# Seven-segment second products for every pair of units, with g's sums made by accumulating DMAs

## The chip, the cores and the metric

The kernel runs on one core of one Trainium2 chip. The metric is the device time of one execution in microseconds (us); the median of several runs counts. A core has a matrix engine (PE, with its weight loads shown as PEld), a vector engine (DVE), an activation engine (ACT), GpSimd (POOL), a queue engine that issues DMAs (SP), and 16 DMA engines that all queues share.

## The reference

Two blocks follow one another. The first is a chunked state-space scan over x (4 batches, 8 heads, 768 steps, 32 channels) with decay `a` and projections B and C (16 states). The second takes the scan's result as 3072 tokens of 256 values through two matrix products with a SiLU between them:

```python
x = attn_out.transpose(0, 2, 1, 3).reshape(B * S, H * D)   # 3072 x 256
h = x @ w_in                                               # 256 x 2048
g = h * (1.0 / (1.0 + np.exp(-h)))
out = g @ w_out                                            # 2048 x 256
```

All is float32.

## The kernel before

**Units and pairs.** The 3072 tokens are cut into 12 units of 256 tokens. For each unit the scan produces XM (the unit's 256 inputs, transposed), the first product gives g in a tile GTS[u] ("gT" in the profile, 128 partitions x 16 blocks of 256), and the second product reads it. Two units form a pair P. Four buffers hold g tiles.

**Seven products in place of eight.** A pair's second product can be seen as a 2 x 2 block product, with blocks of w_out and four blocks of g: b11 and b21 from the pair's first unit, b12 and b22 from its second, where the first index is the half of the 2048 (block number even or odd). Done directly it takes eight block products; with sums of blocks formed beforehand seven are enough. The kernel does the pairs 1 to 5 that way: `s2_pair` (L559) yields after each of 7 segments x 8 matmuls of 128 x 256. The sums of w_out blocks (SO, `f_SO`, L512) are made once on DVE. The sums of g blocks are TN and three in-place ones, made by `f_TS` (L534), each as eight subtractions of 128 x 256, on POOL (the last pair's late ones on DVE). Pair 0, that is units 0 and 1, does its second product directly in `s2_list` (L490): 2 units x 2 halves x 16 matmuls. The first product of units 4 to 11 also has seven segments (`f_x1`, L647), with sums SW of w_in blocks (`f_SW`, L623, POOL) and XT of inputs (`f_XT`, L634, POOL); units 0 to 3 use the direct `f_s1` (L475).

**Order.** Every engine's order is written out by hand. First comes a start-up part in which PE also runs matmuls without use (`busy`, L218), so that it isn't idle. Then w_in and w_out are brought into a reduced form piece by piece (`w_size` on ACT, `w_bits` on DVE and POOL), beside the scans and first products of units 0 to 2. Two loops of eight steps follow, one for unit 2's first product (L838, called loop 1 below) and one for unit 3's (L853, loop 2). Each step takes four PE matmuls of `f_s1` and four of the second product by `f_s2(4)`, and the scan pieces of units 3 (loop 1) and 4, 5 (loop 2): "T" transposes, "E" the decay scans, "B"/"D"/"C" products on POOL, "G" the score matmuls with the state updates `f_S` and the mask products `f_M` on DVE, "Y" the scan's output matmuls and XM. Last come stages G = 2 to 5 (L868), one for each pair's first product: a step j of `f_x1` interleaves its seven matmuls with seven of the previous pair's second product (the "s" in `ORDER`). A final loop (L894) does the last pair alone.

**Queues and buffers that matter.** The scan's scores and output share one PSUM tile "gy" with a single buffer: `f_M` reads the scores there, and `f_Y` (L444) then writes the same place:

```python
nc.vector.tensor_tensor(out=m[:, k], in0=DP[u][:, :, 128 * k:128 * k + 128], in1=m[:, k], op=ALU.mult)
y = ps_s.tile([128, 4, 512], FP32, name="gy")
```

The second product's PSUM tile "o_ps" has one buffer; it is emptied by ACT copies to "ps" tiles (five buffers), which POOL adds (`p_add`, L544) into outputs that DVE transposes and SP stores (`f_out`, L547). SP also issues all loads of a unit (`load_unit`, L124).

Of the kernel before, what the change touches and what calls it, by code (L numbers as in the profile page):

```python
# [21 lines left out]
def kernel(  # L22
# [22 lines left out]
    nc = tc.nc  # L45
# [196 lines left out]
    busy(4, 14)  # L242
# [230 lines left out]


    def f_s1(g, j):  # L475
        if j == 0:
            GTS[g] = gpool.tile([128, NF, UT], FP32, name="gT")
        xm = XM[g].rearrange("p (w c) t -> p w (c t)", w=2)
        hp = ps_h.tile([128, 2, UT], FP32, name="hp")
        for i in range(2):  # L480
            f = 2 * j + i
            for kc in range(KC):
                nc.tensor.matmul(out=hp[:, i], lhsT=w_in_sb[:, kc, f * 128:(f + 1) * 128],  # L483
                                 rhs=xm[:, kc], start=(kc == 0), stop=(kc == KC - 1))
        nc.scalar.activation(GTS[g][:, 2 * j:2 * j + 2], hp, AF.Silu)  # L485
        if j == 7:
            XM.pop(g)


    def s2_list(units):  # L490
        for g in units:
            b, t0 = at(g)
            r = out[b * S + t0:b * S + t0 + UT].rearrange("(k c i) m -> k i c m", k=2, c=2)
            o = ps_o.tile([128, 2, d_model], FP32, name="o_ps")
            for c in range(2):
                for f in range(NF):
                    nc.tensor.matmul(out=o[:, c], lhsT=GTS[g][:, f, 128 * c:128 * c + 128], rhs=w_out_sb[:, f, :],  # L497
                                     start=(f == 0), stop=(f == NF - 1), skip_group_check=True)
                    if f == NF - 1 and c == 1:
                        for e in range(2):  # L500
                            o_sb = ppool.tile([128, UT], FP32, name="ps")
                            nc.scalar.activation(o_sb, o[:, e], AF.Copy)
                            for k in range(2):
                                nc.sync.dma_start(out=r[k][:, e], in_=o_sb[64 * k:64 * k + 64])
                    yield

# [3 lines left out]
    SO, TN, PEND = [], {}, []  # L510

    def f_SO(i):  # L512
# [4 lines left out]
        def new():  # L517
            if i == 3:
                return lo(spare(None, 128))
            return [wtp.tile([128, 2, WF], FP32, name=n).rearrange("p a (b m) -> p (a b) m", m=128)  # L520
                    for n in ("wu", "wv")]

        SO.append(new())
        b = lambda k, m: lo(wjo[:, k, m])
        a0, a1, op = ((b(0, 1), b(1, 1), ALU.add), (SO[0], b(0, 0), ALU.subtract),
                      (b(0, 0), b(0, 1), ALU.subtract), (b(1, 0), SO[min(i, 1)], ALU.subtract))[i]
# [3 lines left out]
    def gb(P, k, v):  # L530

        return GTS[2 * P + v].rearrange("p (j k) t -> p k j t", k=2)[:, k]

    def f_TS(P, i, q, engine):  # L534


        if i == 0 and q == 0:
            TN[P] = tpool.tile([128, NF // 2, UT], FP32, name="TN")
        b11, b21, b12, b22 = gb(P, 0, 0), gb(P, 1, 0), gb(P, 0, 1), gb(P, 1, 1)
        o, a0, a1 = ((TN[P], b12, b11), (b11, b22, TN[P]), (b12, b22, b12), (b21, b21, b11))[i]  # L540
        for j in (2 * q, 2 * q + 1):
            engine.tensor_tensor(out=o[:, j], in0=a0[:, j], in1=a1[:, j], op=ALU.subtract)  # L542

    def p_add(o, p, q, engine):  # L544
        engine.tensor_tensor(out=o, in0=p, in1=q, op=ALU.add)  # L545
# [13 lines left out]
    def s2_pair(P, final=False):  # L559
# [3 lines left out]
                ("5", lambda j: SO[0][j // 4][:, j % 4], lambda: TN[P]),  # L563
                ("6", lambda j: SO[1][j // 4][:, j % 4], lambda: gb(P, 0, 0)),
                ("7", lambda j: SO[2][j // 4][:, j % 4], lambda: gb(P, 0, 1)),
                ("4", lambda j: wjo[:, 1, 1, j], lambda: gb(P, 1, 0)),
                ("3", lambda j: SO[3][j // 4][:, j % 4], lambda: gb(P, 1, 1)))
        for n, (m, w, g) in enumerate(segs):
            if final and n % 2 == 0:
# [3 lines left out]
            for j in range(NF // 2):  # L573
                nc.tensor.matmul(out=o, lhsT=w(j), rhs=g()[:, j], start=(j == 0), stop=(j == NF // 2 - 1))  # L574
                if j == NF // 2 - 1:

                    p[m] = ppool.tile([128, UT], FP32, name="ps")
                    on = o.rearrange("p (c k t) -> p c k t", c=2, k=2)
                    pn = p[m].rearrange("p (k c t) -> p c k t", c=2, k=2)
                    if not (final and m == "3"):  # L580
                        nc.scalar.activation(pn, on, AF.Copy)  # L581
                    if m == "w":
                        p_add(p["w"], p["w"], p["1"], adder)
                        PEND.append(partial(f_out, P, 0, 0, p["w"]))
                    elif m == "6":
                        p_add(p["6"], p["6"], p["1"], adder)
                    elif m == "7":
                        p_add(p["7"], p["7"], p["6"], adder)
                        p_add(p["6"], p["6"], p["5"], adder)
                        p_add(p["5"], p["5"], p["7"], adder)  # L590
                        PEND.append(partial(f_out, P, 1, 1, p["5"]))
                    elif m == "4":
                        p_add(p["4"], p["4"], p["7"], adder)
                        PEND.append(partial(f_out, P, 1, 0, p["4"]))
                    elif m == "3" and final:

                        for k in range(2):
                            nc.vector.tensor_tensor(out=pn[:, :, k], in0=on[:, :, k],
                                                    in1=p["6"].rearrange("p (k c t) -> p c k t", c=2, k=2)[:, :, k],
                                                    op=ALU.add)  # L600
                            f_out(P, 0, 1, p["3"], (nc.sync, nc.scalar), (128 * k, 128 * k + 128))
                    elif m == "3":
                        p_add(p["3"], p["3"], p["6"], adder)
                        PEND.append(partial(f_out, P, 0, 1, p["3"]))
# [18 lines left out]
    def f_SW(i):  # L623
# [5 lines left out]
        nc.gpsimd.tensor_tensor(out=t, in0=a0, in1=a1, op=op)  # L629
# [17 lines left out]
    def f_x1(G, j, dve, act):  # L647
        u0, u1 = 2 * G, 2 * G + 1
        if j == 0:
            for u in (u0, u1):  # L650
                GTS[u] = gpool.tile([128, NF, UT], FP32, name="gT")
# [23 lines left out]
        for what in ORDER[j]:  # L675
# [5 lines left out]
            elif what == "1":  # L681
                mm(X, wj[:, 0, 0, j], b0[:, 0])
                p1 = copy("p1", X)
                add(g0[:, 2 * j], W, p1)
# [4 lines left out]
            elif what == "6":  # L689
                mm(X, SW[1][:, j], t[:, 1], False)  # L690
                u2 = copy("u2", X)
                silu(g0[:, 2 * j], g0[:, 2 * j])
                other(dve, first)
            elif what == "7":
                mm(X, SW[2][:, j], t[:, 2], False)
                add(g1[:, 2 * j + 1], X, p5)
                silu(g1[:, 2 * j + 1], g1[:, 2 * j + 1])
            elif what == "4":
                mm(X, wj[:, 1, 1, j], t[:, 3], False)
                silu(g0[:, 2 * j + 1], X)  # L700
                other(dve, 2)
            elif what == "3":
                mm(Y, SW[3][:, j], b1[:, 1], False)
                add(g1[:, 2 * j], Y, u2)
                silu(g1[:, 2 * j], g1[:, 2 * j])
# [66 lines left out]
    busy(0, 24)  # L772
    f_G0(0)
    busy(4, 10)
# [14 lines left out]
    busy(3, 30)  # L789
# [47 lines left out]
    S2.append(s2_list((0, 1)))  # L837
    for j in range(8):  # L838
        f_s1(2, j)
        scan_piece(3, j, ("", "", "T", "E", "BS", "G", "S", "Y"))  # L840
        f_s2(4)
        if j < len(late):
            w_steps(late[j])
        if j in (2, 5):
            load_unit(4 + j // 3)

    def sums(P, qs):

        for q in qs:
            f_TS(P, 0, q, nc.gpsimd)  # L850
            f_TS(P, 2, q, nc.gpsimd)

    for j in range(8):  # L853
        f_s1(3, j)
# [78 lines left out]
```

## Time and profile before

| | us |
|---|---|
| median of 11 runs | 357.24 |
| lowest, highest | 356.71, 359.27 |
| the profiled execution: its time | 357.97 |
| the profiled execution: its span | 356.2 |

About 1.8 us of a run lie outside the span. Some groups of the page's fifth part (line, engine, operation, tiles and shape, count, then busy us and mean ns of one, then the idle time before):

```profile
L483 PE MATMUL hp<-XM,w_in_sb 128*128 128x256 f32 x256 | 59.3, 381 | 0.7 <-ACT XM L472 0.7
L497 PE MATMUL o_ps<-w_out_sb,gT 128*128 128x256 f32 x128 | 30.9, 384 | 0.0
L545 POOL TENSOR_TENSOR ps<-ps 128x256 f32<-128x256 f32 x28 | 20.3, 728 | 25.9 <-ACT ps L581 12.7
```

A float32 matmul stands in the profile as two records, so the 128 records of L497 are 64 matmuls. Records overlap, as matmuls are pipelined: the mean ns of one record is longer than the distance between two, and busy time is counted without overlap.

### The profile page before, as it was taken

The page shows a single profiled execution, that of the slowest core. Times are in us where ns is not written, and L with a number is a line of the kernel's source. Part 1 is how long each engine was busy: PE and PEld are TensorE (multiplying, and loading weights), DVE is VectorE, ACT ScalarE, POOL GpSimd, SP SyncE. Part 2 cuts the span into 40 slices and gives each one's busy share as a digit, 9 for nine tenths or more (in the row PEclk, how much of TensorE's full clock was granted, in tenths as well). Part 3 has the DMA queues.
Part 4 walks back from the last instruction along what each step waited for, and adds up shares of the span by engine and source line. Part 5 has one row for each costly group of instructions (what it writes and reads, how often), then busy time and mean ns, then how long its engine had stood idle before and what let it go on. Part 6 is the DMA issues. An engine that isn't in the chain of part 4 may idle for free.

```text
span 356.2 us, 8462 instructions
## 1 busy us (share of the span) xinstructions
PE 346.7 (97%) x3353; PEld 292.0 (82%) x3353; DVE 183.4 (51%) x389; ACT 160.4 (45%) x390; POOL 181.7 (51%) x246
## 2 busy tenths in 40 slices
PE   8799999999999999999999999999999999999994
PEld 4478888888888888888888888888888888888883
DVE  6988999554447444543454633455632221214722
ACT  2469576223222545545544545544545454453100
POOL 4425344524059086498274398264398930596100
PEclk9999999999999999999999999999999999999998
DMA  6998967773653251252026153110101100101203
GB/s 107 217 346 136 284 211 129 126 119 72 114 124 45 67 97 17 46 99 37 15 61 106 38 97 45 18 16 2 17 2 16 17 15 0 17 0 21 41 0 45
DMA packets 110059, 26.53 MB, mean 74 GB/s; under 512 B 98884, under 2 KB 105796, under 8 KB 110020
## 3 DMA queue, kind: packets, MB, share of 16 engines
q1 hardware_dynamic: 107044, 25.67, 35.0%
q10 hardware_dynamic: 2976, 0.33, 0.6%
q8 instruction: 26, 0.43, 0.5%
q14 instruction: 13, 0.11, 0.1%
HBM read 22.83 MB, written 3.15 MB: 73 GB/s over the span
## 4 chain that ended last, share of the span: by engine, by line
PE 92%; DMA 2%; DVE 2%; issue 1%; SPq 0%; ACT 0%; ACTq 0%; DVEq 0%
PE o_ps L574 30%; PE hp L657 28%; PE hp L483 15%; PE o_ps L497 8%; PE hp L574 3%; PE gy L463 3%; PE gy L454 2%; PE gy L400 2%; DMA gT<-in_a_dram 1%; PE gy L385 1%; DVE E L411 1%; DMA tbc<-in_B_dram 1%; DVE st L426 0%; DMA out_dram<-ot 0%; DVE gT L275 0%
## 5 line engine op out<-in xcount | busy, mean ns | idle before, releaser
L660 DVE TENSOR_TENSOR gT<-hp,p 128x256 f32<-128x256 f32 x64 | 26.9, 421 | 84.6 <-ACT p L671 47.5
L483 PE MATMUL hp<-XM,w_in_sb 128*128 128x256 f32 x256 | 59.3, 381 | 0.7 <-ACT XM L472 0.7
L663 ACT ACTIVATE gT<-gT 128x256 f32<-128x256 f32 x96 | 39.7, 414 | 42.8 <-DVE gT L660 42.8
L336 POOL TENSOR_TENSOR BT<-bn,E 128x256 f32<-128x256 f32 x12 | 8.8, 736 | 95.1 <-PE hp L657 29.7
L574 PE MATMUL o_ps<-gT,w_out_sb 128*128 128x256 f32 x224 | 56.5, 379 | 0.0
L483 PEld LDWEIGHTS hp<-XM,w_in_sb 128*128 128x128 f32 x256 | 48.1, 190 | 8.1 <-issue 0.9
L657 PE MATMUL hp<-raw 128*128 128x256 f32 x192 | 52.7, 380 | 0.0
L542 POOL TENSOR_TENSOR gT<-gT 128x256 f32<-128x256 f32 x72 | 51.2, 739 | 0.0
L574 PEld LDWEIGHTS o_ps<-gT,w_out_sb 128*128 128x128 f32 x224 | 42.4, 190 | 5.9
L657 PEld LDWEIGHTS hp<-raw 128*128 128x128 f32 x192 | 36.2, 190 | 5.4 <-POOL ps L545 0.6
L671 ACT ACTIVATE p<-hp 128x256 f32<-128x256 f32 x64 | 24.6, 384 | 27.5 <-PE hp L657 25.7
L485 ACT ACTIVATE gT<-hp 128x512 f32<-128x512 f32 x32 | 19.1, 596 | 39.3 <-PE hp L483 39.2
L660 DVE TENSOR_TENSOR gT<-hp,u 128x256 f32<-128x256 f32 x32 | 13.6, 425 | 40.7 <-PE hp L657 40.7
L657 PE MATMUL hp<-XM,w_in_sb 128*128 128x256 f32 x128 | 34.1, 389 | 0.0
L545 POOL TENSOR_TENSOR ps<-ps 128x256 f32<-128x256 f32 x28 | 20.3, 728 | 25.9 <-ACT ps L581 12.7
L497 PE MATMUL o_ps<-w_out_sb,gT 128*128 128x256 f32 x128 | 30.9, 384 | 0.0
L542 POOL TENSOR_TENSOR TN<-gT 128x256 f32<-128x256 f32 x40 | 28.7, 740 | 0.0
L497 PEld LDWEIGHTS o_ps<-w_out_sb,gT 128*128 128x128 f32 x128 | 23.8, 190 | 3.8 <-issue 0.5
L657 PEld LDWEIGHTS hp<-XM,w_in_sb 128*128 128x128 f32 x128 | 23.3, 190 | 4.3 <-issue 1.0
L299 DVE TENSOR_TENSOR_SCAN E<-ab,diag 128x256 f32<-128x256 f32 (+1 forms) x32 | 24.5, 805 | 3.7 <-PE gy L463 3.3
L542 POOL TENSOR_TENSOR gT<-gT,TN 128x256 f32<-128x256 f32 x32 | 22.2, 733 | 0.0
L581 ACT ACTIVATE ps<-o_ps 128x256 f32<-128x256 f32 x31 | 11.9, 384 | 18.5 <-PE o_ps L574 18.1
(123 smaller groups left out, 548.7 us busy)
## 6 DMA issues: line engine op xcount, KB each, us to landing
ab<-in_a_dram SPq DMA_DIRECT2D x40, 128.0 KB, 3.4
raw<-in_moe_w_in_dram SPq DMA_DIRECT2D x8, 512.0 KB, 8.7
raw<-in_moe_w_out_dram SPq DMA_DIRECT2D x8, 512.0 KB, 5.7
xt<-in_x_dram SPq DMA_DIRECT2D x24, 128.0 KB, 4.2
out_dram<-ot SPq DMA_DIRECT2D x76, 32.0 KB, 1.7
bn<-in_B_dram SPq DMA_DIRECT2D x22, 64.0 KB, 5.4
tbc<-in_C_dram SPq DMA_DIRECT2D x40, 32.0 KB, 1.9
pa<-in_a_dram SPq DMA_DIRECT2D x10, 128.0 KB
```

Source lines behind the costliest of these rows:

```text
L299: nc.vector.tensor_tensor_scan(out=E[u].rearrange("p k h t -> p (k h t)")[:, Q * g0:Q * (g0 + n)], data0=t.rearrange("p g t -> p (g t)"), ...
L483: nc.tensor.matmul(out=hp[:, i], lhsT=w_in_sb[:, kc, f * 128:(f + 1) * 128], rhs=xm[:, kc], start=(kc == 0), stop=(kc == KC - 1))
L485: nc.scalar.activation(GTS[g][:, 2 * j:2 * j + 2], hp, AF.Silu)
L497: nc.tensor.matmul(out=o[:, c], lhsT=GTS[g][:, f, 128 * c:128 * c + 128], rhs=w_out_sb[:, f, :], start=(f == 0), stop=(f == NF - 1), skip_ ...
L542: engine.tensor_tensor(out=o[:, j], in0=a0[:, j], in1=a1[:, j], op=ALU.subtract)
L545: engine.tensor_tensor(out=o, in0=p, in1=q, op=ALU.add)
L574: nc.tensor.matmul(out=o, lhsT=w(j), rhs=g()[:, j], start=(j == 0), stop=(j == NF // 2 - 1))
L581: nc.scalar.activation(pn, on, AF.Copy)
L657: nc.tensor.matmul(out=o, lhsT=w, rhs=x_, start=start, stop=True, skip_group_check=True)
L660: nc.vector.tensor_tensor(out=o, in0=p, in1=q, op=ALU.add)
L663: nc.scalar.activation(o, i, AF.Silu)
L671: nc.scalar.activation(o, i, AF.Copy)
```

## The change

- Pair 0's second product is also done by `s2_pair`, with `joint=True`: its first two segments run block by block side by side in the two halves of one PSUM tile, the other five one after the other. `s2_list` is gone. Loop 1 and loop 2 take 2 or 4 matmuls of it in a step, 28 in each.
- The signs of the sums are changed so that all sums of g are additions in place: TN = b12 + b11 (`f_T1`, DVE, in four parts of 128 x 512), then b12 += b22 ("3"), b11 += b12 ("2"), b21 += b11 ("4"). The in-place ones are DMAs with `accum_op`, issued on POOL's queue, each in two halves of 512 KB; the last pair's late ones are DVE or POOL additions of 128 x 1024. The segments "6" and "7" change places.
- g's layout in its tile becomes half first, block second (`new_g`), so that four blocks of a half lie together.
- SW is made on DVE, and spread over loop 2. SO is made in loop 1 (three) and loop 2 (one). Unit 3's scan pieces move: transposes to the end of step 2, "DC" in step 4, "G" at the end of step 6, and "Y" after the first product of step 7 and ahead of the second product's matmuls. Loads are issued after a step's outputs.
- `busy` counts change: (4, 14) to (5), (0, 24) to (0, 20), (4, 10) to (4, 8), (3, 30) to (4, 17), where the first number counts matmuls of 512 columns and the second of 64.

```diff
-    busy(4, 14)
+    busy(5)
...
+    def new_g():
+        return gpool.tile([128, NF, UT], FP32, name="gT").rearrange("p (k j) t -> p k j t", k=2)
...
-        nc.scalar.activation(GTS[g][:, 2 * j:2 * j + 2], hp, AF.Silu)
+        nc.scalar.activation(GTS[g][:, :, j], hp, AF.Silu)
...
+    def f_T1(P, q, engine=nc.vector):
+        if q == 0:
+            TN[P] = tpool.tile([128, NF // 2, UT], FP32, name="TN")
+        js = slice(2 * q, 2 * q + 2)
+        engine.tensor_tensor(out=TN[P][:, js], in0=gb(P, 0, 1)[:, js], in1=gb(P, 0, 0)[:, js], op=ALU.add)
+
+    def f_TS(P, i, h, engine=None):
         b11, b21, b12, b22 = gb(P, 0, 0), gb(P, 1, 0), gb(P, 0, 1), gb(P, 1, 1)
-        o, a0, a1 = ((TN[P], b12, b11), (b11, b22, TN[P]), (b12, b22, b12), (b21, b21, b11))[i]
-        for j in (2 * q, 2 * q + 1):
-            engine.tensor_tensor(out=o[:, j], in0=a0[:, j], in1=a1[:, j], op=ALU.subtract)
+        js = slice(4 * h, 4 * h + 4)
+        o, a = {3: (b12, b22), 2: (b11, b12), 4: (b21, b11)}[i]
+        if engine is None:
+            nc.gpsimd.dma_start(out=o[:, js], in_=a[:, js], accum_op=ALU.add)
+        else:
+            engine.tensor_tensor(out=o[:, js], in0=a[:, js], in1=o[:, js], op=ALU.add)
...
+    def s2_pair(P, final=False, joint=False):
...
+            elif m == "6":
+                p_add(p["6"], p["6"], p["1"], adder)
+                p_add(p["7"], p["7"], p["6"], adder)
+                p_add(p["6"], p["5"], p["6"], adder, ALU.subtract)
+                p_add(p["5"], p["5"], p["7"], adder, ALU.subtract)
+                PEND.append(partial(f_out, P, 1, 1, p["5"]))
...
+        if joint:
+            o = ps_o.tile([128, 2, UT], FP32, name="o_ps")
+            for j in range(NF // 2):
+                for n, (m, w, g) in enumerate(segs[:2]):
+                    nc.tensor.matmul(out=o[:, n], lhsT=w(j), rhs=g()[:, j], start=(j == 0 and n == 0), stop=(j == last),
+                                     skip_group_check=True)
+                    if j == last and n == 1:
+                        end("1", o[:, 0])
+                        end("w", o[:, 1])
+                    yield
...
-        nc.gpsimd.tensor_tensor(out=t, in0=a0, in1=a1, op=op)
+        nc.vector.tensor_tensor(out=t, in0=a0, in1=a1, op=op)
...
-    busy(0, 24)
+    busy(0, 20)
     f_G0(0)
-    busy(4, 10)
+    busy(4, 8)
...
-    busy(3, 30)
+    busy(4, 17)
...
-    S2.append(s2_list((0, 1)))
+    def outputs(todo):
+        for what in todo:
+            what()
+
+    S2.append(s2_pair(0, joint=True))
     for j in range(8):
+        waiting, PEND[:] = PEND[:], []
         f_s1(2, j)
-        scan_piece(3, j, ("", "", "T", "E", "BS", "G", "S", "Y"))
-        f_s2(4)
+        if j == 7:
+            scan_piece(3, 0, "Y")
+        f_s2(2 if j < 2 else 4)
         if j < len(late):
             w_steps(late[j])
+        if j == 2:
+            scan_piece(3, 0, "T")
+            for q in range(4):
+                f_T1(0, q)
+        if j == 3:
+            f_SO(0)
+        scan_piece(3, j, ("", "", "", "E", "DC", "", "G", ""))
+        if j in (5, 6):
+            f_SO((2, 1)[j - 5])
+        outputs(waiting)
...
+        for h in range(2):
+            if j in (3, 5, 7):
+                f_TS(0, {3: 3, 5: 2, 7: 4}[j], h)
...
     for j in range(8):
         f_s1(3, j)
-        scan_piece(4, j, ("TE", "BS", "G", "Y", "", "", "", ""))
-        scan_piece(5, j, ("", "", "T", "E", "BS", "G", "Y", ""))
+        scan_piece(4, j, ("TE", "DCS", "G", "YS", "", "", "", ""))
+        scan_piece(5, j, ("", "", "T", "E", "DCS", "G", "YS", ""))
...
-        f_s2(4)
+        f_s2(2 if j in (5, 6) else 4)
+        if j == 3:
+            f_SO(3)
+        outputs(waiting)
         if j == 5:
-            sums(1, (0, 1))
+            f_T1(1, 0)
+            f_T1(1, 1)
+            f_TS(1, 3, 0)
...
+            if j < 2:
+                f_T1(G - 1, 2 + j)
+            for i, h in {1: ((2, 0), (3, 1)), 2: ((2, 1),), 3: ((4, 0), (4, 1))}.get(j, ()):
+                f_TS(G - 1, i, h)
+            if j == 5:
+                f_T1(G, 0)
+                f_T1(G, 1)
+                f_TS(G, 3, 0)
...
-    sums(P, (3,))
+    f_T1(P, 2)
+    f_T1(P, 3)
+    f_TS(P, 3, 1, nc.gpsimd)
     S2.append(s2_pair(P, True))
...
-            for q in range(4):
-                f_TS(P, 2 * n + 1, q, nc.vector)
+            for h in range(2):
+                f_TS(P, 2 * n + 2, h, nc.vector)
```

## The prediction

> **What bounds the kernel.** I read the page's busy times and its chain first, then busy time by stage (cut where the loops begin), then PE's waits, then the timelines around the places that the change moves.
>
> ```profile
> PE 346.7 (97%) x3353; PEld 292.0 (82%) x3353; DVE 183.4 (51%) x389; ACT 160.4 (45%) x390; POOL 181.7 (51%) x246
> PE 92%; DMA 2%; DVE 2%; issue 1%; SPq 0%; ACT 0%; ACTq 0%; DVEq 0%
> ```
>
> The chain that ended last is PE for 92% of the span, and the other engines are half idle. By stage (start:end, length, busy us of PE, PEld, DVE, ACT, POOL, granted clock, DMA share, GB/s):
>
> ```profile
> 0.00:27.42 27.42, 22.82 (x437) 14.76 (x438) 21.82 (x45) 12.21 (x25) 10.68 (x23) 1.00 0.87 227
> 53.10:83.52 30.42, 30.42 (x283) 26.11 (x281) 20.57 (x34) 10.91 (x21) 11.87 (x9) 1.00 0.70 118
> 83.52:116.87 33.35, 33.35 (x442) 28.08 (x441) 17.52 (x30) 9.61 (x20) 18.06 (x18) 1.00 0.47 89
> 116.87:170.72 53.85, 53.85 (x537) 45.94 (x536) 24.84 (x61) 27.41 (x74) 34.48 (x51) 1.00 0.32 60
> ```
>
> These are the start-up, loop 1, loop 2 and stage G = 2. PE is busy without a gap from 27.42 us until the last matmul (about 351); the only idle PE time is in the start-up. So a matmul taken out behind 27.42 us shortens the run by its full length, unless PE is made to wait somewhere new. Its length comes from the chain of waits: "327.16 3.45 PE hp L574 x16" is one segment, 16 records or 8 matmuls: 0.431 us each. (Check: loops 1 and 2 last 63.8 us; their 128 matmuls take 55.2, and the rest is two to three units' scan matmuls.)
>
> **Pair 0 in seven segments.** Out go L497's 64 matmuls, in come 7 x 8 = 56: 8 x 0.431 = **-3.45 us**, all on PE's path. The number of `f_s1` and scan matmuls stays.
>
> **Sums of g.** POOL loses 144 operations of L542 at 0.73 to 0.74 us, 102 us of its 182. It was no bound, so this gains nothing. DVE gets 24 `f_T1` of 128 x 512. The nearest row is L528, the same shape from SBUF to SBUF on DVE: 0.67 to 1.21 us each, so 16 to 29 us in all. In stages 2 to 5 four of them (2.7 to 4.8 us) come on top of DVE's 25 of 54 us (12 of 49 in the last). Each stands at the end of a step, and behind it waits the step's first g addition (L660), which only has to free a PSUM buffer for the step after. Cost 0; with that cover gone, one `f_T1`'s length (1.2 us) in a step.
>
> In the last loop DVE does four additions of 128 x 1024 instead of 16 of 128 x 256 (7.0 us), and POOL one (L629 has that shape: 2.35 us). Segment "7" needs the POOL result three segments (10.4 us) after the stage; two `f_T1` and that addition take under 5. Cost 0. The tail behind the last matmul is unchanged.
>
> **The accumulating DMAs** are the large unknown: 31 of 512 KB. The trace has none. Nearest row by size:
>
> ```profile
> raw<-in_moe_w_out_dram SPq DMA_DIRECT2D x8, 512.0 KB, 5.7
> ```
>
> 5.7 us to landing, up to seven in line; the DMA view over 22.7 to 24 us shows 389 GB/s, thus 1.35 us of the rings for one. An accumulation has to read two streams and write one. I take two to three times 1.35, that is 2.7 to 4 us each (estimate). Allowance: a stage issues b11 (first half) and b12 (second half) behind step 1, the other half of b11 behind step 2, both of b21 behind step 3. Steps last 54 / 8 = 6.7 us and carry seven second-product matmuls. The fourth of these DMAs is needed at matmul 40, in step 5, some 24 us behind step 1: 6 us each even if all ran one after the other. Cost 0; the loss begins at 6 us each.
>
> The Trainium skill has rules that speak against this step. "DMA: Bandwidth & Descriptors" (Rules for kernel authors) says that an accumulation's destination isn't held while it is read and written back, so that dependent ones must wait for each other's semaphores: b12, then b11, then b21, with POOL's queue standing still at each wait. "SBUF — State Buffer" (SBUF: two separate sides) says that DMAs issued from GpSimd can't write their descriptors while DVE holds the shared port. The trace agrees that DVE and POOL get in each other's way: L176's 128 x 512 pass takes 0.43 us at 25.33 and 1.39 at 29.98, beside a POOL addition. But such a hold lasts one operation, about 1 us: 6 holds a stage would use 6 of the 24 us, while without the rule they use none. Both leave the sum at 0. Behind POOL's waits stand unit products (L336), output additions and XT, all needed a step or more later.
>
> **SW and SO.** Four SW of 128 x 1024 go from POOL (2.35 us) to DVE: twice L528, 1.3 to 2.4 us each, and three SO go from loop 2 to loop 1. DVE's loop 1 by its rows: last weight piece done at about 61.5; transposes 1.2, four `f_T1` 3.3 (66), SO 1.6 (67.7), unit 3's decay scan 4.1 (71.8). PE wants TN and SO at 70.4 and the scan's result (plus 0.7 for L336) at about 75.5. Both hold by 2.5 us. In loop 2 the same count leaves DVE 1 to 2 us ahead of unit 5's "G" with the short durations and 1.5 us late with the long ones. POOL is emptier now, so I take the short ones: 0, with +1.5 as the far end.
>
> **Unit 3's Y is moved too near to its G.** In loop 1 of before:
>
> ```profile
> 72.67 0.69 PE L400 MATMUL gy<-ce,bh 32*64 32x128 f32 x32
> 73.47 0.23 DVE L424 COPY st<-gy 128x64 f32<-128x64 f32 x1 [5.93 <-PE gy L400]
> 73.73 0.91 DVE L426 SCALAR_TENSOR_TENSOR st<-st,pfx,gy 128x64 f32<-128x64 f32 x3
> 74.56 1.28 DVE L411 TENSOR_TENSOR E<-gy,E 128x512 f32<-128x512 f32 x2
> ...
> 80.39 0.58 PE L454 MATMUL gy<-cw,sm 32*64 32x64 f32 x24
> ```
>
> G's matmuls give PE free at 73.29; DVE then needs until 75.84 for states and masks, and Y may not write "gy" sooner. Before, Y came 7.1 us behind G. Now G ends step 6, and between it and Y stands only step 7's first product: 4 x 0.431 = 1.73 us. Needed: 75.84 - 73.29 = 2.55, plus 0.1 from DVE's end to PE's start (unit 1: 24.96 to 25.11). PE waits **+0.9 us**, once. Units 4 (cover 3.45) and 5 (cover 2.6, with a shorter state update that needs 2.3) don't wait.
>
> **The start-up.** One wait there has no releaser:
>
> ```profile
> PE gy L463 <- issue: 2.2, 1, 2.2
> PE o_ps L221 <- DVE gT L216: 1.3, 1, 1.3
> PE hp L483 <- ACT XM L472: 0.7, 1, 0.7
> PE gy L454 <- DVE E L411: 0.4, 2, 0.3
> ```
>
> PE stops in the middle of unit 0's Y (14.43 to 16.61 us). The DMA view over 13.9 to 15.4 us has one 16 KB packet on an instruction queue, beside rings that are busy with weights; the next is at 22.8, the next at 28.1. I read this as PE running out of code. The new `busy` counts take out 31 of 89 matmuls (62 instructions), so the code present reaches 62 instructions further: past the remaining 25 of Y's matmuls, into unit 0's first product, which can't start before its weights at 16.3 anyway. Y(0) then ends at 14.9, not 17.0. DVE begins unit 1's scan 0.3 us sooner (its weight pieces end at 16.86), PE reaches unit 1's state matmuls at 20.7 instead of 21.94, and Y(1) starts about 1.2 us sooner. But the next chunk of code, present from about 25.2 us if its packet comes when it did, is now first needed inside Y(1), at 24.8: 0.5 us are lost again. Net **-0.7 us**. From the two sides: -1.2 if the second chunk is in time; +1.3 if its fetch is asked for by position in the code and not by time, for then the whole 2.2 us hole stands in Y(1), on the path. I take the middle one because both packets are served late, in step with the rings' load.
>
> **The sum** on the profiled execution: span 356.2 - 3.45 + 0.9 - 0.7 = 352.95; with the 1.8 us outside, 354.7 against its 357.97. The median of the runs is 0.7 below that execution, so 357.24 - 3.25 = **354.0 us**.
>
> **Rivals.**
> - *No new waits (0.15).* PE hides Y(3) because step 7's silu and DVE overlap better than I count, and the second chunk is in time: 357.24 - 3.45 - 1.2 = 352.6. For it: DVE is half idle. Against it: the gy buffer's single copy.
> - *Given back (0.13).* The hole moves into Y(1) (+1.3), Y(3) waits (+0.9), and DVE, crowded by SW at its long durations, is late for unit 5 (+1.5): 357.24 + 0.25, about 357.5. For it: the DVE stretch of 17.5 us in loop 2 would grow to about 25.
> - *The accumulating DMAs decide (0.16), slower.* In stages 2 to 5 PE waits at segments "6" and "4" if one takes over 6 us. At 6.6 us the fifth comes about 3.5 us late in each of four stages: 354.0 + 14 = 368. For it: no such transfer is in the trace, and POOL stands in line for each. Against it: the rings are 67 to 93% idle there.
>
> **The numbers.** The forecast has 0.56, with its own range 353.2 to 355.2. Runs of this kernel tell about 0.3% (1.07 us) from no change. Faster: 0.56 + 0.15 + 0.04 of the third case's spread = 0.75. Same: 0.07, the middle of that case. Slower: 0.16 + 0.02 = 0.18. The 8-in-10 range goes from the second case's end, 352.4, to the third's, 357.3; what lies above is mostly the DMAs' case.
>
> **What would show it.** L497 gone and 672 records of second-product matmuls in all (112 a pair, six pairs); loops 1 and 2 together about 61.2 us, that is 63.8 - 3.45 + 0.9; a PE wait of 0.9 on DVE L411 ahead of L454 in unit 3; no "issue" wait in unit 0's Y, a short one in unit 1's; first matmul of unit 1's first product at about 26.7 instead of 27.42; stages of 53.9 us as before, with no PE wait on a DMA. Wrong would be: stages longer than 54 us with PE waiting for gT (the DMAs), or a start-up later than 27.4.

## The result and the profile after

The changed kernel takes 355.04 us (median of 13 runs, 354.53 to 356.96), the kernel before 357.46 beside it: a ratio of 0.9923, with a 95% interval of 0.9903 to 0.9944. That is faster by 2.4 us, by the medians, where I forecast 3.25; the interval of the ratio stands for 2.0 to 3.5 us, so the two can't be told apart by the times alone, and what follows compares terms in the profiles. The profiled execution took 354.87 us, its span is 353.2 (before: 356.2).

The page of the changed kernel, busy times, a DMA queue that before did not have, the chain, and one DMA issue row (KB each, median us to landing):

```profile
PE 342.3 (97%) x3306; PEld 287.1 (81%) x3306; DVE 205.9 (58%) x409; ACT 162.0 (46%) x393; POOL 112.0 (32%) x137
...
q0 software_dynamic: 4464, 16.25, 24.9%
...
PE 91%; DVE 4%; DMA 2%; issue 1%; ACT 0%; POOL 0%; SPq 0%; ACTq 0%; DVEq 0%
...
gT<-gT POOLq DMA_DIRECT2D x31, 512.0 KB, 6.1
```

PE has 47 records fewer: 16 are the 8 matmuls of pair 0, 31 are `busy` matmuls. POOL has lost 70 us and PE's share of the chain is what it was, so POOL's 70 us were not on the path as such. The new queue holds the rings for 24.9% of 353.2 us, 88 us for 31 transfers, thus 2.84 us of all rings each; from issue to landing one takes 6.1.

Busy time by stage (start:end, length, busy us of PE, PEld, DVE, ACT, POOL, granted clock, DMA share, GB/s); the rows are the start-up, loop 1, loop 2 and stage G = 2:

```profile
0.00:26.23 26.23, 21.80 (x407) 13.22 (x407) 21.64 (x45) 12.33 (x25) 11.06 (x23) 1.00 0.87 229
51.90:82.30 30.40, 29.70 (x279) 25.44 (x278) 26.41 (x44) 12.06 (x24) 13.64 (x14) 1.00 0.89 157
82.30:112.87 30.57, 30.57 (x429) 25.61 (x428) 21.99 (x33) 9.88 (x21) 15.40 (x15) 1.00 0.80 134
112.87:166.75 53.88, 53.88 (x537) 45.83 (x536) 28.00 (x66) 27.24 (x73) 15.78 (x22) 1.00 0.80 141
```

Read against the rows of before, this says where the 3.0 us of span are. Up to loop 1 it is 1.2 us earlier (53.10 to 51.90). The two loops last 60.97 us in place of 63.77: 2.80 less. From stage 2 to the last matmul it is 234.19 against 234.09, no change, although the rings in stage 2 are now busy 80% of the time where they were 32%. From the start of the last matmul to the end it is 6.09 against 5.26, 0.83 lost. 1.2 + 2.8 - 0.1 - 0.83 = 3.07.

PE's waits in the changed kernel (waited for: us in total, times, longest):

```profile
PE o_ps L221 <- DVE gT L216: 1.3, 1, 1.3
PE hp L487 <- POOL w_in_sb L182: 1.3, 2, 1.0
PE gy L454 <- ACT gT L489: 0.7, 1, 0.7
PE hp L487 <- ACT XM L472: 0.7, 1, 0.7
PE gy L400 <- ACT ce L361: 0.6, 1, 0.6
PE gy L454 <- DVE E L411: 0.5, 1, 0.5
```

The 2.2 us with no releaser are gone; a smaller hole is left in unit 1's Y (below). In their place stand waits for a weight piece (L182) and for CE (L361), both in the start-up. No row names a DMA or a sum of g. The third row is the new wait in loop 1; its surroundings in the timeline:

```profile
74.92 0.69 PE L400 MATMUL gy<-ce,bh 32*64 32x128 f32 x32
...
76.82 1.28 DVE L411 TENSOR_TENSOR E<-gy,E 128x512 f32<-128x512 f32 x2
...
78.25 0.58 PE L454 MATMUL gy<-cw,sm 32*64 32x64 f32 x24 [0.70 <-ACT gT L489]
```

This is unit 3: scores, masks, then Y. The masks on "gy" end at 78.10 and Y starts 0.15 later, the same distance as in unit 1 of before; the silu that the view names (L489, 77.58 to 78.18) ends at nearly the same time. Which of the two holds Y is tried below.

### The profile page after: what moved, and what is told of

It reads as the page before. It is cut to its first block, busy times and chain, and to the rows that moved or that the text cites. A ratio compares the mean times of both kernels' runs of the same rounds, so it can differ in the third digit from the quotient of the medians.

```text
span 353.2 us, 8347 instructions
## 1 busy us (share of the span) xinstructions
PE 342.3 (97%) x3306; PEld 287.1 (81%) x3306; DVE 205.9 (58%) x409; ACT 162.0 (46%) x393; POOL 112.0 (32%) x137
## 3 DMA queue, kind: packets, MB, share of 16 engines
q0 software_dynamic: 4464, 16.25, 24.9%
## 4 chain that ended last, share of the span: by engine, by line
PE 91%; DVE 4%; DMA 2%; issue 1%; ACT 0%; POOL 0%; SPq 0%; ACTq 0%; DVEq 0%
PE o_ps L614 35%; PE hp L669 28%; PE hp L487 15%; PE hp L614 3%; PE gy L463 3%; PE o_ps L600 2%; PE gy L454 2%; PE gy L400 2%; DVE E L299 1%; PE gy L385 1%; DVE wv L178 1%; DMA tbc<-in_C_dram 1%; DMA tbc<-in_B_dram 1%; DMA out_dram<-ot 0%; DVE gT L275 0%
## 5 line engine op out<-in xcount | busy, mean ns | idle before, releaser
L614 PE MATMUL o_ps<-gT,w_out_sb 128*128 128x256 f32 x240 | 60.4, 379 | 0.0
L540 POOL TENSOR_TENSOR ps<-ps 128x256 f32<-128x256 f32 x35 | 29.4, 839 | 73.8 <-ACT ps L571 72.5
L614 PEld LDWEIGHTS o_ps<-gT,w_out_sb 128*128 128x128 f32 x240 | 45.4, 190 | 6.3
L535 POOL DMA_DIRECT2D gT<-gT x31 | 27.2, 914 | 67.3 <-DVE TN L526 21.5
L489 ACT ACTIVATE gT<-hp 128x512 f32<-128x512 f32 x32 | 19.1, 596 | 30.1 <-PE hp L487 29.9
L299 DVE TENSOR_TENSOR_SCAN E<-ab,diag 128x256 f32<-128x256 f32 (+1 forms) x32 | 25.6, 843 | 0.4
L571 ACT ACTIVATE ps<-o_ps 128x256 f32<-128x256 f32 x38 | 14.5, 383 | 23.9 <-PE o_ps L614 21.0
L336 POOL TENSOR_TENSOR BT<-bn,E 128x256 f32<-128x256 f32 x12 | 9.5, 793 | 46.7 <-DVE E L299 41.4
L614 PE MATMUL o_ps<-gT,wu 128*128 128x256 f32 x88 | 22.2, 380 | 0.0
L614 PE MATMUL o_ps<-gT,wv 128*128 128x256 f32 x88 | 22.2, 380 | 0.0
L614 PE MATMUL o_ps<-gT,raw 128*128 128x256 f32 x80 | 20.6, 382 | 0.0
L669 PE MATMUL hp<-raw,w_in_sb 128*128 128x256 f32 x64 | 19.1, 380 | 0.0
```

The source lines that it names most:

```text
L299: nc.vector.tensor_tensor_scan(out=E[u].rearrange("p k h t -> p (k h t)")[:, Q * g0:Q * (g0 + n)], data0=t.rearrange("p g t -> p (g t)"), ...
L489: nc.scalar.activation(GTS[g][:, :, j], hp, AF.Silu)
L535: nc.gpsimd.dma_start(out=o[:, js], in_=a[:, js], accum_op=ALU.add)
L540: engine.tensor_tensor(out=o, in0=p, in1=q, op=op)
L669: nc.tensor.matmul(out=o, lhsT=w, rhs=x_, start=start, stop=True, skip_group_check=True)
```

## The experiments

Unless said otherwise each is the changed kernel with one edit; "before" is run beside each on the same chip.

### What pair 0's seven segments are worth

`pair0_direct`: pair 0's second product in 64 matmuls again, no sums for it.

```diff
-    S2.append(s2_pair(0, joint=True))
+    S2.append(s2_list((0, 1)))
...
-        f_s2(2 if j < 2 else 4)
+        f_s2(4)
```

> The changed kernel with pair 0's second product done directly, 64 matmuls instead of 56, four in each step of both loops; pair 0's sums of g are left out, everything else as changed. Theory (a matmul on PE's path costs its full 0.431 us): 3.45 us longer than the changed kernel, 358.5, all of it in the two loops. Rival (the seven segments bring waits of their own, so that part of the gain is given back in the loops): less than 3 us longer.

Measured: 358.70 us, ratio 1.0022 (1.0002 to 1.0043). In its trace the two loops take 3.45 us longer than in the changed kernel, which is 8 matmuls of 0.431 to the last digit. The medians lie 3.66 us apart. (The profiled execution is the longest of the twelve, 360.87 us, and comes to loop 1 another 2.95 us later: its start-up has a longer hole in unit 1's Y, and behind it the first product's next 64 records (from 27.48) take 15.75 us, where the changed kernel needs 14.08, at a granted clock of 0.58 from 27 to 30 us.) So this part is worth 3.5 us, and without it the change would not be faster at all.

### The start-up

`old_busy`: the four counts of `busy` as before.

```diff
-    busy(5)
+    busy(4, 14)
```

(and the other three alike)

> The changed kernel with the filler counts of before (89 filler matmuls instead of 58), all else as changed. Theory (the fillers only decide where PE runs out of code): PE's wait of about 2.2 us without a releaser is back in the middle of unit 0's Y, unit 1's first product starts at about 27.4 us again instead of 26.2, and the run is 1.2 us longer than the changed kernel (356.2). Rival (the gain of the start-up comes from something else, such as a warmer clock or other transfers): within 0.3 us of the changed kernel, and unit 1's first product still at about 26.2.

Measured: 355.65 us, 0.9941 (0.9918 to 0.9965): 0.6 slower than the changed kernel in the median, though the intervals overlap. Its timeline has the hole in unit 0's Y again:

```profile
13.50 0.64 PE L463 MATMUL gy<-E,xt 64*32 64x64 f32 x38
15.98 0.43 PE L463 MATMUL gy<-E,xt 64*32 64x64 f32 x26 [1.84 <-issue]
```

Y stops behind the same 38th record as in before (14.43 there), so the place goes with the count of instructions ahead of it.

`before_new_busy`: the other way round, the kernel before with the new counts only.

```diff
-    busy(4, 14)
+    busy(5)
```

(and the other three alike)

> The kernel before with nothing changed but the four counts of busy (those of the changed kernel): 31 matmuls fewer in the start-up. Theory 'the code hole goes with the counts': the issue wait of 2.2 us in unit 0's Y goes, unit 1's first product comes 0.6 to 1.2 us earlier than 27.4, and the run is 0.6 us shorter, 356.8 us, as putting the old counts back into the changed kernel made it 0.6 longer. Theory 'it is something else in the change that closes the hole' (the order of the code behind the start-up): the hole stays and the time is 357.4.

Measured: 357.13 us against 357.50, 0.9976 (0.9953 to 0.9998). Y of unit 0 is now whole, and a smaller hole stands in unit 1's Y:

```profile
24.78 0.30 PE L463 MATMUL gy<-E,xt 64*32 64x64 f32 x4
25.97 0.81 PE L463 MATMUL gy<-E,xt 64*32 64x64 f32 x60 [0.89 <-issue]
```

In this profile unit 1's first product comes at 27.47, no earlier than before. The changed kernel has the second hole too, but short: its unit 1's Y takes 1.22 us where unit 0's takes 0.86.

```profile
24.32 1.22 PE L463 MATMUL gy<-E,xt 64*32 64x64 f32 x64
```

In all twelve profiles with the new counts this hole stands behind the same fourth record of unit 1's Y, which again ties the place to the count. Its length differs from run to run (from one record's start to the next 0.3 us in the changed kernel, 0.5 in `g3_early`, 1.1 here, 1.3 in `pair0_direct`), and the new waits for weight pieces give some back. So the counts are worth 0.4 to 0.6 us in the median, by intervals that hardly separate it from nothing. The -1.2 of the one profile is not all theirs: 0.47 us of it lie ahead of unit 0's Y (13.79 to 13.32), and with the counts alone that place moves by only 0.1 to 0.2 (13.79 to 13.69, 13.50 to 13.32).

### The wait of unit 3's Y

`g3_early`: unit 3's G ahead of step 6's second-product matmuls, not behind them, so that four more stand between G and Y.

```diff
+        if j == 6:
+            scan_piece(3, 0, "G")
         f_s2(2 if j < 2 else 4)
...
-        scan_piece(3, j, ("", "", "", "E", "DC", "", "G", ""))
+        scan_piece(3, j, ("", "", "", "E", "DC", "", "", ""))
```

> The changed kernel with unit 3's score matmuls one group earlier in step 6 of loop 1, ahead of the four second-product matmuls, so that 3.45 us of matmuls stand between G and Y instead of 1.73. Theory (Y waits for DVE's states and masks on the single gy buffer): the PE wait of 0.65 us ahead of unit 3's Y is gone and the loops last 60.3 instead of 61.0 us; run about 354.4. Rival (Y waits for something else, such as the silu of step 7 that the wait is put down to): the wait stays and the time is unchanged.

Measured: 354.63 us, 0.9916 (0.9885 to 0.9947). The wait is gone:

```profile
78.10 0.58 PE L454 MATMUL gy<-cw,sm 32*64 32x64 f32 x24
```

Here the masks are done at 77.00, and step 7's silu runs only from 78.21 to 78.81, after Y has begun. So Y doesn't wait for that silu, which the view had named; what held it was DVE on the single "gy". From the PE group that leads into loop 1 (start 50.17; here 50.80) to stage 2 the time falls from 62.70 to 61.93, 0.77 less. The whole run gains 0.4 in the median, within what the intervals can't tell apart; this profile's hole in unit 1's Y is 0.2 us longer than the changed kernel's.

### The sums of g

`sums_pool`: the in-place sums by POOL additions of 128 x 1024, no accumulating DMA.

```diff
-        if engine is None:
-            nc.gpsimd.dma_start(out=o[:, js], in_=a[:, js], accum_op=ALU.add)
+        if True:
+            (engine or nc.gpsimd).tensor_tensor(out=o[:, js], in0=a[:, js], in1=o[:, js], op=ALU.add)
```

> The changed kernel with all sums of g in place made by POOL additions of 128 x 1024 (31 of 2.35 us, 73 us) in the places where the DMAs are issued, no accumulating DMAs. Theory (the sums are off PE's path whether a DMA or POOL makes them, and the gain is pair 0's eight matmuls): no change, within 0.5 us of the changed kernel. Rival (POOL was the bound of the seven-segment pairs, and the DMAs are what made pair 0's possible): PE waits for gT in the loops or stages, 2 us or more longer.

Measured: 357.87 us, 1.0015 (0.9990 to 1.0039), 2.8 slower than the changed kernel, so that nothing is left of the gain. That is the rival's size, but not its reason: PE doesn't wait for gT. The stages are as long as before (53.9); the loss is in the loops, in two waits of PE of 1.3 us each for BT, the unit product that the scores read (units 3 and 4). Unit 3's wait, and POOL ahead of it:

```profile
76.41 0.46 PE L385 MATMUL gy<-xt,BT 64*32 64x64 f32 x32 [1.31 <-POOL BT L336]
...
67.40 2.67 POOL L535 TENSOR_TENSOR gT<-gT 128x1024 f32<-128x1024 f32 x1 [0.69 <-DVE TN L526]
70.03 1.18 POOL L538 TENSOR_TENSOR ps<-ps 128x256 f32<-128x256 f32 x1
75.50 0.86 POOL L336 TENSOR_TENSOR BT<-bn,E 128x256 f32<-128x256 f32 x1 [4.29 <-PE o_ps L612]
```

It looks as if BT stood behind POOL's additions, but POOL is idle for 4.3 us ahead of it, and the PE instruction named had no data for it. What BT reads comes from DVE:

```profile
62.27 4.99 DVE L526 TENSOR_TENSOR TN<-gT 128x512 f32<-128x512 f32 x4
67.18 0.68 DVE L515 TENSOR_TENSOR wu<-w_out_sb 128x512 f32<-128x512 f32 x1
67.78 2.84 DVE L515 TENSOR_TENSOR wv<-w_out_sb 128x512 f32<-128x512 f32 x1
...
72.94 2.34 DVE L299 TENSOR_TENSOR_SCAN E<-ab,diag 128x512 f32<-128x512 f32 x2
```

and in the changed kernel:

```profile
61.78 2.84 DVE L526 TENSOR_TENSOR TN<-gT 128x512 f32<-128x512 f32 x4
64.54 0.68 DVE L515 TENSOR_TENSOR wu<-w_out_sb 128x512 f32<-128x512 f32 x1
65.15 0.68 DVE L515 TENSOR_TENSOR wv<-w_out_sb 128x512 f32<-128x512 f32 x1
...
67.60 2.83 DVE L299 TENSOR_TENSOR_SCAN E<-ab,diag 128x512 f32<-128x512 f32 x2
```

The same DVE addition takes 0.68 us, or 2.84 where a POOL addition of 2.67 runs beside it; four `f_T1` take 4.99 for 2.84. So the scan E ends at 75.28, not at 70.43, and BT follows it by 0.2 us, as in the changed kernel (70.65). POOL's additions cost the path nothing by POOL's own time; they hold up DVE. The Trainium skill's rule ("SBUF — State Buffer", SBUF: two separate sides) that a DVE operation with two inputs from SBUF and a GpSimd operation lock each other out for a whole instruction fits these numbers.

`sums_late`: the stages' five DMAs one step later.

```diff
-            for i, h in {1: ((2, 0), (3, 1)), 2: ((2, 1),), 3: ((4, 0), (4, 1))}.get(j, ()):
+            for i, h in {2: ((2, 0), (3, 1)), 3: ((2, 1),), 4: ((4, 0), (4, 1))}.get(j, ()):
```

> The changed kernel with stages 2 to 5 issuing the accumulating DMAs one step (about 7 us) later. Theory (one transfer takes 6 to 8.6 us to landing, each link of the chain b12, b11, b21 waits for the one before, and the data are ready about 6 us before PE reads them): PE begins to wait ahead of segments 7 and 6, 0.5 to 2 us in a stage, run 2 to 8 us longer than the changed kernel. Rival (the slack is far more than a step, as the prediction's 24 us for four transfers of 3 to 4 us would have it): no change.

Measured: 354.95 us, 0.9924 (0.9900 to 0.9948): no change. The last ones are issued at 145 us in place of 135.6 and 142.0, and PE still waits for none. So the data were not near their limit in the changed kernel. This left open what was.

`sum4_twice`: segment 4's two sums made twice in the stages, so that its g is b21 + 2 b11.

```diff
                 f_TS(G - 1, i, h)
+                if i in (4,):
+                    f_TS(G - 1, i, h)
```

> In stages 2 to 5 the two halves of b21 + b11 (segment 4's g) are each added twice, so that the last link of the chain is two accumulating DMAs longer; the output then has b21 + 2 b11 in that segment. By the trace of the changed kernel the sums land about 6 us before they are read (in stage 2: landed by 146, first read at 151), and one takes about 4.5 us from issue when little else runs. Theory 'room of 6 us': one dependent repeat fits, both halves in line (9 us) don't: PE waits 1 to 3 us on a DMA ahead of segment 4 in each of the four stages, 359 to 367 us. Theory 'far more room' : no change from the changed kernel, 355.0. Theory 'already at the edge' (my forecast's 6 us per transfer, with 6.1 measured): at least 4.5 us a stage, 373 us or more.

Measured: 382.89 us, 1.0717 (1.0656 to 1.0778). The number fits the third theory (373 us or more), its reason doesn't: all three were about the data, and PE waits only 0.5 us in all for the transfers. It waits for BT. First the changed kernel in stage 2, POOL and then PE:

```profile
134.77 1.76 POOL L535 DMA_DIRECT2D gT<-gT  x2 [5.41 <-PE hp L669]
142.02 0.85 POOL L535 DMA_DIRECT2D gT<-gT  x1 [5.48 <-PE o_ps L614]
143.60 0.64 POOL L336 TENSOR_TENSOR BT<-bn,E 128x256 f32<-128x256 f32 x1 [0.74 <-DVE E L299]
...
145.90 0.46 PE L385 MATMUL gy<-xt,BT 64*32 64x64 f32 x32
```

and the same place in `sum4_twice`:

```profile
144.79 1.75 POOL L535 DMA_DIRECT2D gT<-gT  x2 [8.31 <-DMA gT<-gT]
153.88 0.86 POOL L535 DMA_DIRECT2D gT<-gT  x1 [7.34 <-DMA tbc<-in_B_dram]
154.44 0.97 POOL L336 TENSOR_TENSOR BT<-bn,E 128x256 f32<-128x256 f32 x1
...
155.47 0.68 PE L385 MATMUL gy<-xt,BT 64*32 64x64 f32 x32 [9.51 <-POOL BT L336]
```

In the changed kernel BT waits 0.74 us for DVE and ends 1.66 us before PE starts on it (145.90 - 144.24). So POOL's last issue can be 0.74 + 1.66 = 2.4 us later, and no more. In `sum4_twice` POOL stands twice ahead of a repeat, 8.3 and 7.3 us (the view puts the first wait down to a sum of g and the second to a load; that the second, too, is for the sum before it follows from the order of the program alone). BT starts 10.8 us later although DVE has its input ready at the same time (143.4), and PE waits 9.5. The waits on BT are 21.9 us in all; the rest of the 28 us is mostly PE's lower clock behind them (below).

`sums_twice`: all five of a stage twice.

```diff
                 f_TS(G - 1, i, h)
+                if i in (2, 3, 4):
+                    f_TS(G - 1, i, h)
```

> All five accumulating DMAs of a stage are issued twice in stages 2 to 5 (segments 2, 3 and 4 then work on wrong multiples of the same blocks), so each costs twice its time in POOL's line and on the rings. Theory 'room of 6 us': 5 repeats of about 4.5 us, two of them side by side, make the last sum 13 to 20 us later, so PE waits 7 to 14 us in each of four stages and POOL holds up its additions of x too: 385 to 410 us, with PE waits put down to DMA gT<-gT or to POOL. Theory 'far more room': 355 to 357 us. This prices the rival in which the DMAs decide.

Measured: 439.91 us, 1.2292 (1.2239 to 1.2345), far beyond 410. Of PE's waits 52.0 us in three are for BT and 18.0 in six for the DMAs themselves.

`sum4_twice_late`: segment 4's sums twice, but a step later, behind BT.

```diff
-            for i, h in {1: ((2, 0), (3, 1)), 2: ((2, 1),), 3: ((4, 0), (4, 1))}.get(j, ()):
+            for i, h in {1: ((2, 0), (3, 1)), 2: ((2, 1),), 4: ((4, 0), (4, 1))}.get(j, ()):
...
+                if i in (4,):
+                    f_TS(G - 1, i, h)
```

> As sum4_twice (segment 4's two sums made twice in stages 2 to 5, so its g holds b21 + 2 b11), but issued one step later, behind POOL's next unit product BT (L336) in place of ahead of it. In sum4_twice PE's 9.5 us wait at 145.9 us was put down to BT, which stood on POOL behind the repeats. Theory 'POOL's line decides, not the data': BT keeps its place (about 143.8 us in stage 2), the waits of PE on BT are gone, and what is left is the data's own lateness: the first half's repeat is issued when its first pass has landed (about 150) and lands at about 155, read at 151.3: about 4 us a stage, put down to DMA gT<-gT or POOL's additions, 371 us (365 to 376). Theory 'the transfers decide' (rings or the data's chain): moving the issue behind BT makes the data later still, so the time is 383 us as for sum4_twice or more.

Measured: 377.76 us, 1.0530 (1.0482 to 1.0578): 5 us less than `sum4_twice` although the same transfers start later. POOL, then PE:

```profile
143.94 0.63 POOL L336 TENSOR_TENSOR BT<-bn,E 128x256 f32<-128x256 f32 x1 [8.20 <-DMA out_dram<-ot]
...
145.16 0.86 POOL L535 DMA_DIRECT2D gT<-gT  x1
150.73 1.74 POOL L535 DMA_DIRECT2D gT<-gT  x2 [4.71 <-DMA gT<-gT]
...
156.24 2.05 PE L614 MATMUL o_ps<-gT,w_out_sb 128*128 128x256 f32 x4 [4.51 <-DMA gT<-gT]
```

BT is in its place, no wait on it is left, and PE now waits for the data where segment 4 begins (151.33 without it): 15.8 us in six waits. The order on POOL's queue is therefore a cause by itself, and the transfers' own lateness another that lies behind it. The size was underestimated, 378 for 371: behind the three longest waits (3.5 to 4.8 us) PE runs slowly for a while, which I had not counted.

### SW, and outputs on another queue

`sw_pool`: SW's four additions on POOL again.

```diff
-        nc.vector.tensor_tensor(out=t, in0=a0, in1=a1, op=op)
+        nc.gpsimd.tensor_tensor(out=t, in0=a0, in1=a1, op=op)
```

> The changed kernel with the four sums SW back on POOL (2.35 us each), in their new places in loop 2. Theory (DVE has 1 to 2 us in hand in loop 2 with SW on it, and POOL stands in line for nothing that PE needs at once): no change within 0.4 us. Rival (crowding on DVE is near the bound and SW's place decides): up to 1.5 us shorter, or longer if POOL's products for units 4 and 5 come late behind SW.

Measured: 356.59 us, 0.9980 (0.9963 to 0.9997), 1.5 slower than the changed kernel, as the rival's last clause had it. PE waits 1.3 us for BT of unit 5 (to 105.7 us). Here it is POOL's order: DVE's scan E is done at 100.7, POOL is busy without a gap with output additions to 102.3, with an SW addition of 2.80 us to 105.0, and then makes BT (105.04), which in the changed kernel starts at 101.59.

`out0_act`: pair 0's 16 output stores issued by ACT, not by SP.

```diff
+        queues = queues or ((nc.scalar,) if P == 0 else None)
```

> The changed kernel with pair 0's 16 output DMAs issued from ACT's queue instead of SP's, 16 instructions less on SP. Theory (SP runs out of code between its last two stores, 349.7 to 350.6 us): the gap goes, since the same place in the code now lies behind the last store; tail from the start of the last matmul 6.1 to 5.2 us, run about 354.2. Rival 1 (the gap is a busy DMA queue): it stays. Rival 2 (the ACT issues hold up silu and copies, 0.4 us each): loop 2 longer by 0.5 to 2 us.

Measured: 378.92 us, 1.0608 (1.0564 to 1.0651), a miss. ACT stood still in loop 1:

```profile
70.26 0.60 ACT L489 ACTIVATE gT<-hp 128x512 f32<-128x512 f32 x1 [1.07 <-PE hp L487]
82.65 4.95 ACTq L550 DMA_DIRECT2D out_dram<-ot  x4
87.65 0.60 ACT L489 ACTIVATE gT<-hp 128x512 f32<-128x512 f32 x1 [16.79 <-DMA out_dram<-ot]
```

The transpose that the first store reads was done at 73.2, yet ACT issued it at 82.65, and a silu of unit 3 behind it came 16.8 us late. PE waited 10.8 us ahead of Y(3). From 72 to 84 us the rings were over 90% busy nearly throughout, by far the most with accumulating DMAs (their queue alone took 79% of the rings' time), and SP was issuing unit loads. What exactly held ACT's first store for 9.4 us is not shown.

`g3_tail`: `g3_early`, and of the last pair's stores six on ACT's queue.

```diff
-                PEND.append(partial(f_out, P, 0, 0, p["w"]))
+                PEND.append(partial(f_out, P, 0, 0, p["w"], (nc.scalar,) if final else None))
...
-                PEND.append(partial(f_out, P, 1, 1, p["5"]))
+                PEND.append(partial(f_out, P, 1, 1, p["5"], (nc.sync, nc.scalar) if final else None))
```

> The changed kernel with unit 3's score matmuls early (as in g3_early) and six of the last pair's output DMAs on ACT's queue instead of SP's, in the final loop, where ACT copies once in 3.45 us. Theory (SP's gap of 0.9 us ahead of its last store is a fetch of its code, whose place in the program moves when SP issues fewer DMAs; pair 0's 16 DMAs off SP left it where it was[...]): the gap goes and the tail falls from 5.9 to about 5.1 us; with the Y wait gone, run about 353.7. Rival (the gap belongs to the last store itself, as it came there with 16 DMAs less too): the tail stays at 5.9 us, run about 354.6.

Measured: 354.39 us (353.85 to 355.08), 0.9914 (0.9886 to 0.9942), the shortest of all kernels here, though its interval overlaps that of the changed kernel. It has no wait ahead of Y(3), and 5.53 us from the start of the last matmul in place of 6.09. The longer tail shows in SP's queue. In the changed kernel:

```profile
348.51 2.40 SPq L549 DMA_DIRECT2D out_dram<-ot  x3
```

The same three issues in the kernel before, and then in `g3_tail`:

```profile
352.40 1.38 SPq L554 DMA_DIRECT2D out_dram<-ot  x3
...
348.06 1.47 SPq L549 DMA_DIRECT2D out_dram<-ot  x3
```

SP pauses ahead of its last store in the changed kernel: that store starts 3.53 us behind the start of the last matmul, in before 2.39, in `g3_tail` 2.48. In the pause (349.05) the DMA view shows one packet on an instruction queue, so I read it as SP's code coming late, like PE's in the start-up; that it is the code was inferred from this packet and not tried by itself. Over the profiles of all kernels here the tail is 5.3 to 6.3 us, and it goes with that packet: in seven of them it comes 1.7 to 2.6 us behind the start of the last matmul, with tails of 5.5 to 6.3; in the other seven, before among them, none comes between the start of the last matmul and the last store, and six of these tails are 5.3 to 5.4 us, one 5.7. The count of SP's instructions alone doesn't decide it: `sum4_twice` has as many for SP as the changed kernel (367 records), but its packet comes 1.1 us ahead of the last matmul's start and its tail is 5.35 us.

## Why the prediction was nearly right

**Pair 0: right, and it carries the result.** Forecast -3.45; `pair0_direct` shows 3.45 in the loops and 3.66 between the medians. The 672 records are there (640 of L614, 32 of L600).

**Sums of g: half right.** DVE's 24 `f_T1` took 18.0 us, 0.78 each, inside the 16 to 29, and cost nothing. But "It was no bound, so this gains nothing" looked at POOL's load alone. `sums_pool` is 2.8 us slower and `sw_pool` 1.5, each by waits on BT in the loops. Additions of 128 x 1024 on POOL held up DVE in the one and BT on POOL's own queue in the other. I had noted that the two engines get in each other's way (0.43 and 1.39 us for one pass), and had used it only against the DMAs, not for the additions that the DMAs replace.

**The accumulating DMAs: the cost of 0 right, the limit wrong.** The rings' time of 2.84 us lies in my 2.7 to 4, the time to landing, 6.1, doesn't: I had priced rings, where what waits is landing. By "the loss begins at 6 us each", worked out for all in line, 6.1 would have been the edge, but `sums_late` shows that the data have room: not all run in line. The real limit is in the sentence "Behind POOL's waits stand unit products (L336), output additions and XT, all needed a step or more later". BT is needed 1.7 us after it is done. In stage 2 POOL's queue had 2.4 us to spare there, and `sum4_twice` with `sum4_twice_late` shows that exceeding it costs at this place first. So the third rival was the right danger, at a place that I had named as harmless. As to the rule of the Trainium skill ("DMA: Bandwidth & Descriptors", Rules for kernel authors) that dependent accumulations wait for one another's semaphore: the trace agrees, POOL stood 18.0 us in five such waits. In the changed kernel they cost nothing; where they grow, the price is paid by what is behind them on the queue. The port hold that I had allowed for, about 1 us an issue, doesn't show: the 31 issues took POOL 0.85 to 1.18 us each.

**SW and SO: right.** DVE's SW took 1.20 to 1.34 us each, the short durations; unit 5 is not late.

**Unit 3's Y: right in place and cause, a little less in size.** 0.7 us for 0.9; `g3_early` takes it away.

**The start-up: right in mechanism.** The hole in unit 0's Y goes, a second one in unit 1's Y comes as forecast, and what the first gives is partly lost again. -0.7 forecast, 0.4 to 0.6 less by the two runs, 1.2 less in the profile; the second hole, forecast at 0.5, is 0.3 in the changed kernel and 0.2 to 1.3 over the twelve profiles. The places go with the count of instructions; that the holes are PE's code coming late rests on the packets alone.

**"The tail behind the last matmul is unchanged": the step that failed.** It is 0.83 us longer in the profile. With 0.83 added and 0.2 taken off for Y(3) the sum of -3.25 becomes -2.6, near the -2.4 of the medians; but one profile of each kernel gives the 0.83, and the interval of 2.0 to 3.5 holds both sums. I had looked for pauses on PE alone, and SP has one too, which in before came where it did no harm (349.62, ahead of the last matmul's start) and now falls ahead of the last store. Why it comes when it does stays open. That the profile's sum of -3.07 is so near the forecast is in part luck: the start-up gave 0.5 us more than forecast and Y(3) cost 0.2 less, which makes up for most of the tail.

## What to carry to other kernels

Before a wait is put on a queue, look up for the very next instructions behind it how long before their use they end: here 2.4 us of room ahead of one unit product decided over 28 us, while the transfers had more. Where a step's data come through DVE, an addition on POOL beside it is priced by what it does to DVE (0.68 us became 2.84), not by POOL's load. And an edit that changes the number of instructions ahead of a place can move a pause that no wait explains, as on PE here: look for such pauses at the start and at the last store, where nothing hides them.

## What the runs showed of the hardware

A long wait of PE costs more than its length. In `sum4_twice`, behind the wait of 9.5 us that ends at 155.4 (columns as in the stage table; the granted clock is the third number from the end):

```profile
155.40:158.00 2.60, 2.53 (x66) 1.95 (x67) 0.00 (x0) 0.00 (x0) 0.64 (x2) 0.50 1.08 180
158.00:162.00 4.00, 4.00 (x12) 3.20 (x12) 2.20 (x7) 0.38 (x1) 0.00 (x0) 0.57 1.15 161
162.00:168.00 6.00, 6.00 (x118) 4.97 (x117) 3.04 (x5) 3.19 (x9) 2.91 (x4) 1.00 0.42 58
```

For 6.6 us after it PE runs at 0.50 to 0.57 of its clock: 2.60 x 0.50 + 4.00 x 0.43, some 3 us lost on top of 9.5. That stage is 12.4 us longer than in the changed kernel, which is the two together. The waits of 0.7 us in the loops of the changed kernel show nothing of this (clock 1.00); in the start-up of `pair0_direct` the hole of 1.3 and a wait of 0.7 us close behind it are followed by a clock of 0.58 over 3 us, but in `before_new_busy`, with 1.1 and 0.7, it stays at 1.00.

An accumulating DMA of 512 KB inside the core's memory takes 2.84 us of the rings, about twice the 1.35 of a load of the same size (at the 389 GB/s of the start-up), and its issue holds POOL for 0.87 us in the median. Rings busy for 80% of stage 2, where they were 32%, didn't slow PE's matmuls: 53.88 us for the stage against 53.85.
